# A delta-rule layer with a feed-forward: one order of the array's quarters, and 32 weight columns instead of 64 in the products between blocks

## The chip, the cores and the metric

The kernel runs on one core of a Trainium2 chip. A core has TensorE (matrix products, in the profile PE, and PEld for its weight loads), VectorE (DVE), ScalarE (ACT), GpSimd (POOL) and SyncE (SP), which issues most of the DMAs. Matmuls read SBUF and write PSUM; VectorE and ScalarE take the results from there. The metric is device time in microseconds. The kernel before takes 687.32 us, the median of three runs from 686.33 to 687.77; the profiled run has a span of 685.1 us.

## The reference

Four batches, eight heads, 768 positions, head size 48. Each head carries a 48x48 state; every position reads it with q, and then writes a corrected value with its normalised k:

```python
for t in range(S):
    kt, vt, bt = (k_n[:, :, t], v[:, :, t], beta[:, :, t, None])
    y[:, :, t] = np.einsum('bhd,bhde->bhe', q[:, :, t], state)
    v_old = np.einsum('bhde,bhd->bhe', state, kt)
    state = state + bt[:, :, :, None] * np.einsum('bhd,bhe->bhde', kt, vt - v_old)
```

The result, as 3072 tokens of 384 features, goes through a feed-forward layer: `h = x @ w_in` (384 to 2048), `g = max(h, 0) + alpha * min(h, 0)`, `g @ w_out` (back to 384). All is fp32.

## The kernel before, in words

The sequence is cut into 12 chunks of 64 positions. One step n works on one chunk of two of the four batches, so there are 24 steps; text and code call a step a batch. The 128 partitions hold two halves t (one for each of the two batches), and the eight heads are four pairs g of two parities a. A small product of 64x64 uses one quarter of the 128x128 array: the half of the partitions that it reads (array rows) and the half that it writes (array columns). Each of the four combinations of a and t goes to a quarter. `quarters()` (L377) lists the 16 products of one operation: over g, then a, then t. Which quarter (a, t) is follows from the slices: `half(t)`, `dims(a)` or `half(t ^ a)` for what is read, and the same for what is written. In `through_state` (L663) it is row a, column t; in `solve` (L683) row t, column t ^ a; in `outputs` (L695) row t ^ a, column t; in `next_state` (L710) row t ^ a, column a.

The recurrence inside a chunk becomes a triangular system for each head. Its 64x64 matrix is split into four blocks of 32 (HB = 32). The two diagonal blocks are inverted by elimination on VectorE (`eliminate`, L470 and L476), for four steps at a time; `placing` puts the inverses into `diag` and `inv`. The block between the two is found by two products: `between_1` (L623) multiplies the block outside the diagonal (`right`) by the first block's inverse and copies the result to `mid` on ScalarE (L634); `between_2` (L638) multiplies `mid` by the second inverse, and VectorE adds the result to `inv` (L650). Both ask for 64 weight columns:

```python
right[n % EARLY][half(t), a * G + g : a * G + g + 2].rearrange("p b i -> p (b i)"),
...
p[half(t), a, g], mid[n % 2][x, a * G + g], diag[n % NE][x, a * G + g, HB:C]
```

Two neighbouring blocks of 32 columns make the 64 of the first, so that the block that matters comes out in the second 32 partitions of a half; the others' results meet zeros in `diag`. Weights are the first input of `nc.tensor.matmul` after the output (L629, L644), 64 columns; the moving operand has 32.

`changes(n)` is true for n > 4: from there on odd heads change halves, and all four quarters are used. For steps 0 to 4 between_1 and between_2 use only two, upper left and lower right.

One step of the main loop is `attention(n)` (L956), in four shares: through_state(n) and between_1(n+1); solve(n), grams(n+8) and between_2(n+1); outputs(n), next_state(n) and grams for q; transposes. `weave` interleaves these shares with the feed-forward of an earlier chunk (`ffn_in` L819, `ffn_out_fast` L883), the placements, and the elimination. Orders on all engines are written out by hand: an instruction waits for what stands ahead of it on its engine. PSUM for small products is `ps_big`, three buffers in turn; the feed-forward has two banks in turn. Its evacuation is a relu on ScalarE (L829) and two multiply-adds on VectorE (L831).

Of the kernel before, what the change touches and what calls it, by code (L numbers as in the profile page):

```python
# [28 lines left out]
ALU = mybir.AluOpType  # L29
# [3 lines left out]
C = 64  # L33
HB = 32
W_IN_P = 512
BUSY = 8
EARLY = 8
# [4 lines left out]
def kernel(  # L42
# [11 lines left out]
    nc = tc.nc  # L54
# [8 lines left out]
    G = H // 2  # L63
# [23 lines left out]
    def half(i):  # L87
        return slice(64 * i, 64 * i + 64)
# [156 lines left out]
    for t in range(2):  # L245
# [5 lines left out]
        out=ones, in_=ones, compare_op=ALU.is_ge, fill=1.0, base=0,  # L251
# [7 lines left out]
    for t in range(2):  # L259
# [5 lines left out]
        out=first_of, in_=ident.rearrange("p (q u e) -> p u q e", u=2, e=HB // 2)[:, 0],  # L265
# [30 lines left out]
    NE = 2  # L296
# [77 lines left out]
        for dst, src in copies:  # L374
            nc.scalar.copy(dst.rearrange("p g i -> p (g i)"), src)  # L375

    def quarters():  # L377
        return [(g, a, t) for g in range(G) for a in range(2) for t in range(2)]

    def grams(n_k, n_q):  # L380

        p = ps_big().rearrange("p a (w g i) -> p a w g i", w=2, g=G)
        for w, n, rhs in ((0, n_k, k_t), (1, n_q, q_t)):
            if n < N:
                for g, a, t in quarters():
                    nc.tensor.matmul(  # L386
                        p[half(t ^ a if w else t), a, w, g], k_t[n][dims(a), g, half(t)],
                        rhs[n][dims(a), g, half(t)],
                    )
        if n_k < N:  # L390
            w = stats[n_k][1][:, 0:2, :, None].to_broadcast([128, 2, G, HB])
            for dst, cols in (
                (gather(n_k), slice(0, HB)), (right[n_k % EARLY][:, 1:], slice(HB, C))
            ):
                nc.vector.tensor_tensor(  # L395
                    out=dst.rearrange("p (a g) i -> p a g i", a=2), in0=p[:, :, 0, :, cols],
                    in1=w, op=ALU.mult,
                )
            keep(n_k)

        if n_q < N:
            a_t[n_q] = work.tile([128, H, C], FP32, name="a_t")
            nc.vector.tensor_tensor(
                out=a_t[n_q].rearrange("p (a g) i -> p a g i", a=2), in0=p[:, :, 1],
                in1=minus[:, None, None, :].to_broadcast([128, 2, G, C]), op=ALU.mult,
            )
# [169 lines left out]
    def changes(n):  # L576

        return n > NJ
# [41 lines left out]

    PLACING = 6

    def between_1(n):  # L623

        if n >= N:
            return
        p = ps_big()[:, :, 0 : G * HB].rearrange("p a (g i) -> p a g i", a=2, g=G)
        for g, a, t in quarters():
            nc.tensor.matmul(  # L629
                p[half(t ^ a if changes(n) else t), a, g],  # L630
                right[n % EARLY][half(t), a * G + g : a * G + g + 2].rearrange("p b i -> p (b i)"),
                diag[n % NE][half(t), a * G + g, 0:HB],
            )
        nc.scalar.copy(  # L634
            mid[n % 2].rearrange("p (a g) i -> p a g i", a=2)[:, :, :, 0:HB], p
        )

    def between_2(n):  # L638
        if n >= N:
            return  # L640
        p = ps_big()[:, :, 0 : G * HB].rearrange("p a (g i) -> p a g i", a=2, g=G)
        for g, a, t in quarters():
            x = half(t ^ a if changes(n) else t)
            nc.tensor.matmul(  # L644
                p[half(t), a, g], mid[n % 2][x, a * G + g], diag[n % NE][x, a * G + g, HB:C]
            )
        to, own = (
            x[n % NE].rearrange("p (a g) i -> p a g i", a=2)[:, :, :, HB:C] for x in (inv, diag)
        )
        nc.vector.tensor_tensor(out=to, in0=to if changes(n) else own, in1=p, op=ALU.add)  # L650


    nv, rhs_, ys, us, xts = {}, {}, {}, {}, {}
# [9 lines left out]
    def through_state(n):  # L663
        c, bp = steps[n]
        if c == 0:
            rhs_[n] = by_parity(nv[n])
            return
        r = work.tile([128, H, D], FP32, name="r")
        p = ps_big()[:, :, 0 : 2 * G * D].rearrange("p a (w g d) -> p a w g d", w=2, g=G)
        for w, x in ((0, k_t), (1, q_t)):  # L670
            for g, a, t in quarters():
                nc.tensor.matmul(  # L672
                    p[half(t), a, w, g], x[n][dims(a), g, half(t)], state[bp][dims(a), t, g]
                )
        nc.vector.tensor_tensor(  # L675
            out=r.rearrange("p (a g) d -> p a g d", a=2), in0=by_parity(nv[n]), in1=p[:, :, 0],
            op=ALU.subtract,
        )
        y = work.tile([128, H, D], FP32, name="y")
        nc.scalar.copy(by_parity(y), p[:, :, 1])  # L680
        rhs_[n], ys[n] = r.rearrange("p (a g) d -> p a g d", a=2), y

    def solve(n):  # L683
        p = ps_big()[:, :, 0 : G * D].rearrange("p a (g d) -> p a g d", a=2, g=G)
        for g, a, t in quarters():
            nc.tensor.matmul(  # L686
                p[half(t ^ a), a, g], inv[n % NE][half(t), a * G + g], rhs_[n][half(t), a, g]
            )
        us[n] = work.tile([128, 2, G, D], FP32, name="u")
        nc.vector.tensor_tensor(  # L690
            out=us[n], in0=p,
            in1=stats[n][1][:, 0:3:2, :, None].to_broadcast([128, 2, G, D]), op=ALU.mult,
        )

    def outputs(n):  # L695
        c, bp = steps[n]
        p = ps_big()[:, :, 0 : G * D].rearrange("p a (g d) -> p a g d", a=2, g=G)
        for g, a, t in quarters():
            nc.tensor.matmul(  # L699
                p[half(t), a, g], a_t[n][half(t ^ a), a * G + g], us[n][half(t ^ a), a, g]  # L700
            )
        if c == 0:
            ys[n] = work.tile([128, H, D], FP32, name="y")
            nc.scalar.copy(by_parity(ys[n]), p)
        else:
            nc.vector.tensor_tensor(
                out=by_parity(ys[n]), in0=by_parity(ys[n]), in1=p, op=ALU.add
            )

    def next_state(n):  # L710
        c, bp = steps[n]
        if c < NCH - 1:
            p = ps_big()[:, :, 0 : G * D].rearrange("p t (g d) -> p t g d", g=G)
            for g, a, t in quarters():
                nc.tensor.matmul(  # L715
                    p[dims(a), t, g], k_late[n % NKL][half(t ^ a), 2 * g + a, 0:D],
                    us[n][half(t ^ a), a, g],
                )
            for a in range(2):
                x = state[bp][dims(a)]  # L720
                nc.vector.tensor_tensor(out=x, in0=x, in1=p[dims(a)], op=ALU.subtract)  # L721
# [315 lines left out]
    def queries():  # L1037

        p = [x.rearrange("p (n g i) -> p n g i", n=2, g=G) for x in ffn_banks]
        for n in range(2):  # L1040
            for g, a, t in quarters():
                nc.tensor.matmul(
                    p[a][half(t ^ a), n, g], k_t[n][dims(a), g, half(t)],
                    q_t[n][dims(a), g, half(t)],
                )
            a_t[n] = work.tile([128, H, C], FP32, name="a_t")
# [259 lines left out]
```

## Time and profile before

| engine | busy us | share | instructions |
|---|---|---|---|
| TensorE matmul (PE) | 664.0 | 97% | 10063 |
| TensorE weight load (PEld) | 573.3 | 84% | 10063 |
| VectorE (DVE) | 461.9 | 67% | 1133 |
| ScalarE (ACT) | 248.8 | 36% | 592 |

| group | count | busy us |
|---|---|---|
| feed-forward in, L819 | 1152 | 269.1 |
| between_1, L629 | 768 | 17.6 |
| between_2, L644 | 768 | 17.4 |
| solve, L686 (both forms) | 768 | 16.4 |
| outputs, L699 | 768 | 16.5 |
| copy to mid, L634 | 24 | 0.38 each |
| sum into inv, L650 | 24 | 0.41 each |

An fp32 matmul shows as two recorded instructions, each with its own weight load, so 24 steps of 16 products are 768; a transpose shows as one. A form such as `64*64 64x32` is array rows * weight columns, and then the output. A row of the timeline merges neighbours of one kind: start, length, engine, line, count; matmuls overlap, so what a group costs is the next group's start less its own. Brackets give idle time of the engine ahead of it and what ended it.

### The profile page before, as it was taken

How to read it: one execution, taken by the hardware profiler on the slowest of the kernel's cores; microseconds unless marked ns; L12 is line 12 of the kernel's file. 1: busy time of each engine (PE TensorE's matmuls, PEld its weight loads, DVE VectorE, ACT ScalarE, POOL GpSimd, SP SyncE). 2: the span in 40 equal slices, each digit the busy share in tenths (PEclk: the TensorE clock that was granted, in tenths of full speed). 3: DMA queues.
4: the chain of work that ended last, by engine and by line, in shares of the span. 5: the costliest groups of instructions: out<-in, count | busy, mean ns of one | idle time of the engine just before them, and what ended most of it. 6: DMA issues, size and time to landing. Idle time of an engine off the chain costs nothing.

```text
span 685.1 us, 22945 instructions
## 1 busy us (share of the span) xinstructions
PE 664.0 (97%) x10063; PEld 573.3 (84%) x10063; DVE 461.9 (67%) x1133; ACT 248.8 (36%) x592; POOL 19.2 (3%) x74
## 2 busy tenths in 40 slices
PE   6989999999999999999999999999999999999997
PEld 4567877666678988988988988988989989989997
DVE  5875799879988378967368967369877255245161
ACT  5936756344434244244234234134034133131110
POOL 4000010000000000000000000000000000000000
PEclk9999999999999999999999999999999999999999
DMA  8847644211412212212212112211211210100000
GB/s 123 237 139 197 161 106 117 69 36 37 78 30 39 40 36 45 41 34 46 37 37 37 36 26 36 38 27 34 48 22 28 54 27 17 31 7 2 24 1 23
DMA packets 110963, 37.76 MB, mean 55 GB/s; under 512 B 104160, under 2 KB 107248, under 8 KB 110864
## 3 DMA queue, kind: packets, MB, share of 16 engines
q1 hardware_dynamic: 109088, 35.81, 24.2%
q8 instruction: 79, 1.29, 0.8%
q10 hardware_dynamic: 1776, 0.49, 0.4%
q14 instruction: 20, 0.16, 0.1%
HBM read 31.56 MB, written 4.72 MB: 53 GB/s over the span
## 4 chain that ended last, share of the span: by engine, by line
PE 82%; DVE 11%; ACT 3%; DMA 1%; issue 1%; ACTq 0%; SPq 0%; DVEq 0%
PE p_ffn L819 35%; PE p_ffn L883 27%; PE p_big L672 3%; PE p_big L386 3%; PE p_big L353 2%; PE p_big L699 2%; PE p_big L686 2%; PE p_big L629 2%; PE p_big L644 2%; DVE block L476 2%; DVE prod L470 2%; DMA ke<-in_k_dram 1%; PE p_big L715 1%; PE p_ffn L861 1%; DVE block L446 1%
## 5 line engine op out<-in xcount | busy, mean ns | idle before, releaser
L819 PE MATMUL p_ffn<-xt,w_in 128*128 128x256 f32 x1152 | 269.1, 385 | 5.1 <-DVE act L831 2.1
L819 PEld LDWEIGHTS p_ffn<-xt,w_in 128*128 128x128 f32 x1152 | 211.8, 190 | 36.1 <-issue 3.6
L831 DVE SCALAR_TENSOR_TENSOR act<-act,al_t,p_ffn 128x256 f32<-128x256 f32 x176 | 76.3, 474 | 71.1 <-ACT act L829 70.7
L829 ACT ACTIVATE act<-p_ffn 128x512 f32<-128x512 f32 x88 | 52.3, 594 | 124.6 <-PE p_ffn L819 124.5
L883 PE MATMUL p_ffn<-w_out,act 128*128 128x192 f32 x480 | 83.7, 328 | 0.0
L883 PEld LDWEIGHTS p_ffn<-w_out,act 128*128 128x128 f32 x480 | 78.6, 190 | 0.9
L476 DVE TENSOR_TENSOR block<-block,prod 128x30 f32<-128x30 f32 (+9 forms) x150 | 49.7, 331 | 5.1
L470 DVE TENSOR_TENSOR prod<-block 128x30 f32<-128x30 f32 (+9 forms) x150 | 48.7, 325 | 2.0
L903 DVE TENSOR_TENSOR o_sb<-u,p_ffn 128x192 f32<-128x192 f32 x40 | 13.2, 351 | 41.7 <-PE p_ffn L883 35.4
L680 ACT COPY y<-p_big 128x384 f32<-128x384 f32 x22 | 10.5, 478 | 69.5 <-DVE r L675 69.5
L375 ACT COPY q_t<-p_big 128x512 f32<-128x512 f32 x24 | 13.9, 589 | 55.8 <-PE p_big L353 55.8
L375 ACT COPY k_t<-p_big 128x512 f32<-128x512 f32 x24 | 13.9, 578 | 54.5 <-PE p_big L353 54.4
L883 PE MATMUL p_ffn<-space_out,sums 128*128 128x192 f32 x160 | 29.3, 326 | 0.0
L883 PE MATMUL p_ffn<-more,sums 128*128 128x192 f32 x160 | 29.3, 326 | 0.0
L883 PE MATMUL p_ffn<-w_out,sums 128*128 128x192 f32 x160 | 27.7, 326 | 0.0
L883 PEld LDWEIGHTS p_ffn<-more,sums 128*128 128x128 f32 x160 | 26.6, 190 | 0.0
L883 PEld LDWEIGHTS p_ffn<-space_out,sums 128*128 128x128 f32 x160 | 26.6, 190 | 0.0
L594 ACT ACTIVATE diag<-inverse,which 64x128 f32<-64x128 f32 (+2 forms) x62 | 25.5, 412 | 2.2 <-DVE inverse L446 1.3
L883 PEld LDWEIGHTS p_ffn<-w_out,sums 128*128 128x128 f32 x160 | 25.8, 190 | 0.0
L434 ACT COPY same<-right 32x256 f32<-32x256 f32 x32 | 12.9, 402 | 34.5 <-DVE right L395 34.4
L721 DVE TENSOR_TENSOR state<-state,p_big 48x384 f32<-48x384 f32 x44 | 24.1, 549 | 1.3 <-PE p_big L715 0.9
L903 DVE TENSOR_TENSOR u<-u,p_ffn 128x192 f32<-128x192 f32 x20 | 7.0, 351 | 25.4 <-PE p_ffn L883 25.4
(155 smaller groups left out, 945.7 us busy)
## 6 DMA issues: line engine op xcount, KB each, us to landing
w_out<-in_moe_w_in_dram SPq DMA_DIRECT2D x12, 512.0 KB, 4.9
qp<-in_q_dram SPq DMA_DIRECT2D x48, 96.0 KB, 3.0
v_raw<-in_v_dram SPq DMA_DIRECT2D x48, 96.0 KB, 3.0
kl<-in_k_dram SPq DMA_DIRECT2D x96, 48.0 KB, 2.6
out_dram<-o_sb SPq DMA_DIRECT2D x92, 48.0 KB, 1.6
space_out<-in_moe_w_out_dram SPq DMA_DIRECT2D x11, 384.0 KB, 4.3
ke<-in_k_dram SPq DMA_DIRECT2D x43, 96.0 KB, 3.5
w_out<-in_moe_w_out_dram SPq DMA_DIRECT2D x5, 384.0 KB, 4.8
```

What stands on the lines that cost most here:

```text
L375: nc.scalar.copy(dst.rearrange("p g i -> p (g i)"), src)
L386: nc.tensor.matmul(p[half(t ^ a if w else t), a, w, g], k_t[n][dims(a), g, half(t)], rhs[n][dims(a), g, half(t)],)
L470: nc.vector.tensor_tensor(out=prod, in0=r[:, 0:j, j : j + 1].to_broadcast([128, j, n]), in1=r[:, j : j + 1, j + 1 : HB].to_broadcast([128, ...
L476: nc.vector.tensor_tensor(out=r[:, 0:j, j + 1 : HB], in0=r[:, 0:j, j + 1 : HB], in1=prod, op=ALU.add)
L594: nc.scalar.mul(dst[n % NE][to or rows, a.start * G : a.stop * G, cols], src[m][rows, heads], which[rows, i : i + 1],)
L672: nc.tensor.matmul(p[half(t), a, w, g], x[n][dims(a), g, half(t)], state[bp][dims(a), t, g])
L721: nc.vector.tensor_tensor(out=x, in0=x, in1=p[dims(a)], op=ALU.subtract)
L819: nc.tensor.matmul(p_h[:, i], w_in[:, t, (f + i) * 128 : (f + i + 1) * 128], xt[:, t], start=(t == 0), stop=(t == KT - 1),)
L829: nc.scalar.activation(g, p_h, ACT.Relu, scale=-1.0)
L831: nc.vector.scalar_tensor_tensor(out=g[:, i], in0=g[:, i], scalar=al_t[:, f + i : f + i + 1], in1=p_h[:, i], op0=ALU.mult, op1=ALU.add,)
L883: nc.tensor.matmul(p, x(i), w(i), start=(i == 0), stop=(i == FP - 1))
L903: nc.vector.tensor_tensor(out=to, in0=x, in1=p, op=ALU.add)
```

## The change

`quarters` now takes two functions, which say what array row and what array column (a, t) has, and sorts the 16 products of an operation by g, row, column. All small products so walk the quarters in one order. For steps 0 to 4, where between_1 and between_2 use two quarters, the sorted order takes each twice in a row.

From step 5 on, between_1 loads only the block that matters, 32 weight columns, and writes only the second 32 partitions of each half; between_2 loads 32 columns of mid and writes only the first 32 partitions. The copy to mid and the sum into inv then touch 32 partitions of each half, so each becomes two instructions. It is meant to shorten weight loads, and to have successive products find free quarters. The arithmetic of what is kept is the same.

```diff
--- before.py
+++ after.py
@@ -374,15 +374,28 @@
         for dst, src in copies:
             nc.scalar.copy(dst.rearrange("p g i -> p (g i)"), src)
 
-    def quarters():
-        return [(g, a, t) for g in range(G) for a in range(2) for t in range(2)]
+    def quarters(row, col):
+
+        return sorted(
+            ((g, a, t) for g in range(G) for a in range(2) for t in range(2)),
+            key=lambda x: (x[0], row(x[1], x[2]), col(x[1], x[2])),
+        )
+
+    def parity(a, t):
+        return a
+
+    def batch_(a, t):
+        return t
+
+    def mixed(a, t):
+        return t ^ a
 
     def grams(n_k, n_q):
 
         p = ps_big().rearrange("p a (w g i) -> p a w g i", w=2, g=G)
         for w, n, rhs in ((0, n_k, k_t), (1, n_q, q_t)):
             if n < N:
-                for g, a, t in quarters():
+                for g, a, t in quarters(parity, mixed if w else batch_):
                     nc.tensor.matmul(
                         p[half(t ^ a if w else t), a, w, g], k_t[n][dims(a), g, half(t)],
                         rhs[n][dims(a), g, half(t)],
@@ -620,34 +633,60 @@
 
     PLACING = 6
 
+    def first_half(t):
+        return slice(64 * t, 64 * t + HB)
+
+    def second_of(t):
+        return slice(64 * t + HB, 64 * t + C)
+
     def between_1(n):
 
         if n >= N:
             return
         p = ps_big()[:, :, 0 : G * HB].rearrange("p a (g i) -> p a g i", a=2, g=G)
-        for g, a, t in quarters():
-            nc.tensor.matmul(
-                p[half(t ^ a if changes(n) else t), a, g],
-                right[n % EARLY][half(t), a * G + g : a * G + g + 2].rearrange("p b i -> p (b i)"),
-                diag[n % NE][half(t), a * G + g, 0:HB],
-            )
-        nc.scalar.copy(
-            mid[n % 2].rearrange("p (a g) i -> p a g i", a=2)[:, :, :, 0:HB], p
-        )
+        to = mid[n % 2].rearrange("p (a g) i -> p a g i", a=2)[:, :, :, 0:HB]
+
+        if changes(n):
+            for g, a, t in quarters(batch_, mixed):
+                nc.tensor.matmul(
+                    p[second_of(t ^ a), a, g], right[n % EARLY][half(t), a * G + g + 1],
+                    diag[n % NE][half(t), a * G + g, 0:HB],
+                )
+            for t in range(2):
+                nc.scalar.copy(to[second_of(t)], p[second_of(t)])
+        else:
+            for g, a, t in quarters(batch_, batch_):
+                x = right[n % EARLY][half(t), a * G + g : a * G + g + 2]
+                nc.tensor.matmul(
+                    p[half(t), a, g], x.rearrange("p b i -> p (b i)"),
+                    diag[n % NE][half(t), a * G + g, 0:HB],
+                )
+            nc.scalar.copy(to, p)
 
     def between_2(n):
         if n >= N:
             return
         p = ps_big()[:, :, 0 : G * HB].rearrange("p a (g i) -> p a g i", a=2, g=G)
-        for g, a, t in quarters():
-            x = half(t ^ a if changes(n) else t)
-            nc.tensor.matmul(
-                p[half(t), a, g], mid[n % 2][x, a * G + g], diag[n % NE][x, a * G + g, HB:C]
-            )
         to, own = (
             x[n % NE].rearrange("p (a g) i -> p a g i", a=2)[:, :, :, HB:C] for x in (inv, diag)
         )
-        nc.vector.tensor_tensor(out=to, in0=to if changes(n) else own, in1=p, op=ALU.add)
+        if changes(n):
+            for g, a, t in quarters(mixed, batch_):
+                x = half(t ^ a)
+                nc.tensor.matmul(
+                    p[first_half(t), a, g], mid[n % 2][x, a * G + g, 0:HB],
+                    diag[n % NE][x, a * G + g, HB:C],
+                )
+            for t in range(2):
+                x = to[first_half(t)]
+                nc.vector.tensor_tensor(out=x, in0=x, in1=p[first_half(t)], op=ALU.add)
+        else:
+            for g, a, t in quarters(batch_, batch_):
+                nc.tensor.matmul(
+                    p[half(t), a, g], mid[n % 2][half(t), a * G + g],
+                    diag[n % NE][half(t), a * G + g, HB:C],
+                )
+            nc.vector.tensor_tensor(out=to, in0=own, in1=p, op=ALU.add)
 
 
     nv, rhs_, ys, us, xts = {}, {}, {}, {}, {}
@@ -668,7 +707,7 @@
         r = work.tile([128, H, D], FP32, name="r")
         p = ps_big()[:, :, 0 : 2 * G * D].rearrange("p a (w g d) -> p a w g d", w=2, g=G)
         for w, x in ((0, k_t), (1, q_t)):
-            for g, a, t in quarters():
+            for g, a, t in quarters(parity, batch_):
                 nc.tensor.matmul(
                     p[half(t), a, w, g], x[n][dims(a), g, half(t)], state[bp][dims(a), t, g]
                 )
@@ -682,7 +721,7 @@
 
     def solve(n):
         p = ps_big()[:, :, 0 : G * D].rearrange("p a (g d) -> p a g d", a=2, g=G)
-        for g, a, t in quarters():
+        for g, a, t in quarters(batch_, mixed):
             nc.tensor.matmul(
                 p[half(t ^ a), a, g], inv[n % NE][half(t), a * G + g], rhs_[n][half(t), a, g]
             )
@@ -695,7 +734,7 @@
     def outputs(n):
         c, bp = steps[n]
         p = ps_big()[:, :, 0 : G * D].rearrange("p a (g d) -> p a g d", a=2, g=G)
-        for g, a, t in quarters():
+        for g, a, t in quarters(mixed, batch_):
             nc.tensor.matmul(
                 p[half(t), a, g], a_t[n][half(t ^ a), a * G + g], us[n][half(t ^ a), a, g]
             )
@@ -711,7 +750,7 @@
         c, bp = steps[n]
         if c < NCH - 1:
             p = ps_big()[:, :, 0 : G * D].rearrange("p t (g d) -> p t g d", g=G)
-            for g, a, t in quarters():
+            for g, a, t in quarters(mixed, parity):
                 nc.tensor.matmul(
                     p[dims(a), t, g], k_late[n % NKL][half(t ^ a), 2 * g + a, 0:D],
                     us[n][half(t ^ a), a, g],
@@ -1038,7 +1077,7 @@
 
         p = [x.rearrange("p (n g i) -> p n g i", n=2, g=G) for x in ffn_banks]
         for n in range(2):
-            for g, a, t in quarters():
+            for g, a, t in quarters(parity, mixed):
                 nc.tensor.matmul(
                     p[a][half(t ^ a), n, g], k_t[n][dims(a), g, half(t)],
                     q_t[n][dims(a), g, half(t)],
```

## The prediction

> **What bounds the kernel now.** I read the page first, for engine totals and the chain that ended last.
>
> ```profile
> PE 664.0 (97%) x10063; PEld 573.3 (84%) x10063; DVE 461.9 (67%) x1133; ACT 248.8 (36%) x592; POOL 19.2 (3%) x74
> PE 82%; DVE 11%; ACT 3%; DMA 1%; issue 1%; ACTq 0%; SPq 0%; DVEq 0%
> ```
>
> TensorE fills 97% of the span and 82% of the chain. An average over stages hides where it is not the limit, so next came busy time in two stretches.
>
> ```profile
> 155.00:213.00 58.00, 54.25 (x1031) 40.91 (x1029) 52.67 (x131) 24.98 (x65) 2.44 (x8) 1.00 0.28 50
> 213.00:637.00 424.00, 423.78 (x6378) 387.09 (x6379) 274.85 (x650) 131.30 (x317) 3.44 (x16) 1.00 0.17 32
> ```
>
> After the stretch, its length come PE, PEld, DVE, ACT and POOL busy. From 213 to 637 us PE is busy 423.78 of 424 us; its only listed wait there is 0.6 us. A nanosecond saved on PE in it is a nanosecond of the end. From 155 to 213 us DVE is busy 52.67 of 58 and PE stands still 3.75: there DVE work counts. Batch 5's between-products start at 170.94 us, batch 6's at 187.05, batch 7's at 215.21. So of the 19 batches that change (5 to 23), 17 lie in the PE-bound part, with two products each: **34 products that count**.
>
> Then the timeline, for what one product costs. Each product is 16 small matmuls, which the profile records as 32 pairs of LDWEIGHTS and MATMUL (two per fp32 matmul).
>
> ```profile
> 446.49 0.56 PEld L672 LDWEIGHTS p_big<-state,k_t 48*64 48x64 f32 x32 [0.23 <-issue]
> 446.95 0.56 PEld L672 LDWEIGHTS p_big<-state,q_t 48*64 48x64 f32 x32
> 447.41 0.56 PEld L629 LDWEIGHTS p_big<-diag,right 64*64 64x64 f32 x32
> 448.02 4.61 PEld L819 LDWEIGHTS p_ffn<-xt,w_in 128*128 128x128 f32 x22
> ...
> 452.96 0.56 PEld L686 LDWEIGHTS p_big<-r,inv 64*64 64x64 f32 x32 [0.33 <-issue]
> 453.42 0.56 PEld L644 LDWEIGHTS p_big<-diag,mid 64*64 64x64 f32 x32
> ```
>
> Subtract starts. L672 already walks the quarters in the new order: 446.49 to 446.95, 0.46 us for 32 pairs. L686 walks them crosswise (upper left, lower right, then the other two): 452.96 to 453.42, also 0.46. The order of four different quarters costs nothing. L629 takes 447.41 to 448.02, 0.61: the same 0.46 plus **0.15 us** until the array takes 128x128 weights. Where the moving operand has 64 columns (L386) the pitch is again about 0.46-0.48; where the weights have 48 columns (L715) it is 0.36. So the columns of the weights set the pitch, not those that stream.
>
> ```profile
> 51.50 0.34 PEld L545 LDWEIGHTS p_big<-turned,sums 32*32 32x32 f32 x32 [0.33 <-issue]
> 51.87 0.30 PEld L819 LDWEIGHTS p_ffn<-xt,w_in 128*128 128x128 f32 x2
> ...
> 74.47 1.01 PEld L644 LDWEIGHTS p_big<-diag,mid 64*64 64x64 f32 x32 [0.33 <-issue]
> 75.52 1.16 PEld L819 LDWEIGHTS p_ffn<-xt,w_in 128*128 128x128 f32 x6
> ```
>
> L545 loads 32 columns into four separate parts of the array, between two stretches of feed-forward: 51.50 to 51.87, **0.37 us** with its own start and its leaving. L644 at 74.47 is batch 2 or 3, which uses two quarters only: 1.05 us, not 0.61, since two quarters share the loads of four.
>
> **What the Trainium skill says.** "TensorE: Matmul & The Clock Gate", section LDWEIGHTS: the load takes time by its columns, columns / 1.2 ns, rows don't matter. For 64 and 32 columns that is 53 and 27 ns. The trace agrees: 0.46 us / 8 rounds of four quarters is 58 ns a round, and the 48-column 0.36 / 8 is 45. "TensorEngine Tiling (Array Packing)", Key Properties: "Changing tiling mode (not just tile) drains the TensorE"; Available Configurations lists 64x32 apart from 64x64. The trace shows such a drain between 64x64 and 128x128 (the 0.15), none between 64x64 and 64x32, since no instruction has 32 columns with 64 rows. The first page's Engine queue depths gives TensorE a window of 64 from which loads are pulled ahead. That four quarters run side by side although each matmul is two recorded pairs fits it; how far it reaches past one quarter's queue no row shows.
>
> **The change part by part.**
>
> *32 columns.* It removes half the weight columns of 34 products that count. Today each takes 0.61 from first load to the feed-forward's first load; with 32 columns I take L545's 0.37: **-0.24**. That is the nearest row: same weight columns, four parts busy; its streams are 16 columns, not 32, but streamed columns did not set the pitch.
>
> *A new switch.* Today L629 follows L672, and L644 follows L386 or L686, in the same 64x64 tiling. After the change the array goes 64x64, 64x32, 128x128. The new switch costs between 0, if the hardware lets the tilings mix, and 0.15, what leaving 64x64 costs now. I take 0.15, because of the skill's sentence. Each product then gains 0.24 - 0.15 = 0.09, and 34 of them **-3.1 us**; without the drain 34 x 0.24 = -8.2.
>
> *Split evacuations.* The copy to mid (L634) and the sum into inv (L650) each become two instructions on 32 partitions. Splitting partitions halves nothing: 128x256 takes L634 0.38, and L434 copies 32x256 in 0.40. So 19 more instructions on ACT and 19 on DVE. From 213 us both hide under PE: ACT is busy 131 of 424 us and DVE 275; behind the second copy on ACT stand the diag placements and the relu L829, behind the second sum on DVE stands the scaling L658, and a feed-forward bank has some 2.6 us (12 recorded matmuls of 0.22) before PE wants it again, against 1.5 for its relu and two sums. In the DVE-bound part the chain has these:
>
> ```profile
> 177.94 0.33 DVE inv L650
> ...
> 190.92 0.28 ACT mid L634
> ...
> 195.80 0.33 DVE inv L650
> ```
>
> Two more sums at 0.33 and one copy of about 0.3: at most 1.0, at least 0 where a gap swallows them. I take **+0.8**.
>
> *Order, four quarters.* grams for q, solve, outputs, next_state, queries: **0**, by the two equal 0.46.
>
> *Order, batches 0 to 4.* Here the new order is upper left twice, lower right twice, where it alternated. If loads pass each other freely it costs nothing; if a quarter's queue holds only one waiting pair, the second quarter starts two rounds (0.12 us) late and ends as late. Ten products, some back to back: 0 to 1.2 us, of which part hides behind ScalarE. I take **+0.4**.
>
> *Sum:* -3.1 + 0.8 + 0.4 = -1.9, and 687.3 - 1.9 = **685.4 us**.
>
> **The rivals.**
>
> *No drain, 680.3 us:* -8.2 + 1.2 = -7.0. For it: 48-row and 48-column products follow the 64x64 ones with no gap (0.36 and 0.46). Against: those use the same quarters, so they are no change of tiling; and the one change the trace shows is paid for every time.
>
> *Eaten up, about 687.3:* the drain takes 0.15, the exit is no cheaper, and DVE in the stretch before 213 us hands on more than two sums. Each product would gain 0.05, 1.7 in all, against 1.2 to 1.8 lost. For it: the gain is a difference of two nearly equal terms. Against: L545's exit is inside its 0.37.
>
> *Slower, 693 us or so, in two ways.* If 64-row tiles with 32 columns load no faster than 64-column ones, 34 products pay the 0.15 for nothing: +5.1 + 1.2, 693.6. No row shows that shape; the 48-column 0.36 speaks against it. Or the doubled quarters of batches 0 to 4 run one after the other: ten products of 1.05 become about 2.0, +9.4, and 687.3 - 3.1 + 0.8 + 9.4 = 694.4. Against it: each matmul is already two pairs in one quarter, and two quarters still overlap.
>
> **How the numbers follow.** Forecast 0.56, no drain 0.22, eaten up 0.08, slower 0.14. The forecast is the likeliest case. Its own bounds are 687.3 - 3.1 + 0 = 684.2 and 687.3 - 3.1 + 2.2 = 686.4. The range must take in the no-drain case, so its low end is 680.0; the high end 688.0 covers eaten up and leaves out the slower cases, 0.14, and a little of the other tails. Two parts in a thousand are 1.4 us: faster means under 685.9. The no-drain case (0.22) and about three quarters of the forecast (0.42) lie there: 0.64. Within: 0.14 of the forecast and eaten up: 0.22. Slower: 0.14.
>
> **What would show it.** Loads of L629's and L644's successors should have the form 64*32 from batch 5 on. The timeline between the last L672 load's group and the next L819 is the test: L672's second group would stretch from 0.46 to about 0.61 (drain), and the new product to feed-forward take 0.37. If L672 stays at 0.46, the no-drain rival holds. If the new product takes 0.6, the slower one does. Starts of L686, L699, L715 to their successors should stay 0.46, 0.46, 0.36. L644 of batches 2 and 3 should stay near 1.05, at worst 1.2; near 2 means that the doubled order serializes. The 213 to 637 stretch should shrink by some 3 us with PE still without waits, and 155 to 213 grow by under 1. Any PE wait on L831 after 213 us would mean that the split evacuations do not hide, and the prediction is wrong there.

## The result, and the profile after

The changed kernel takes **690.39 us** (median of 4 runs, 690.21 to 692.47) against 687.55 us (686.33 to 687.82) for the kernel before, run beside it: a ratio of 1.0052, 95% interval 1.0029 to 1.0074. The forecast was 685.4 us with a range up to 688.0; the change makes the kernel slower.

First the page of the kernel after, the engine totals and the chain by engine:

```profile
PE 663.9 (96%) x10063; PEld 568.9 (83%) x10063; DVE 471.2 (68%) x1152; ACT 259.9 (38%) x611; POOL 19.4 (3%) x74
PE 78%; DVE 13%; ACT 4%; SPq 2%; issue 1%; DMA 1%; DVEq 0%; ACTq 0%
```

PEld fell from 573.3 to 568.9, so weights are loaded faster, as meant. DVE grew by 9.3 us and ACT by 11.1 us, with 19 more instructions each. The chain gives TensorE 78% where it gave 82%, VectorE 13% where it gave 11%. Now the same two stretches of the kernel after:

```profile
155.00:213.00 58.00, 52.45 (x1024) 38.64 (x1023) 52.38 (x129) 25.72 (x66) 1.50 (x6) 1.00 0.24 45
213.00:637.00 424.00, 421.63 (x6367) 381.21 (x6366) 284.41 (x669) 141.40 (x335) 4.50 (x18) 1.00 0.17 33
```

PE stands still for 2.4 us of the long stretch; before it was 0.2 us. In the short one it stands still for 5.6 us, where it was 3.75. These are the waits of TensorE after 213 us, from the list of waits of PE and of the weight loads:

```profile
PE p_ffn L922 <- DVE act L870: 1.0, 2, 0.5
PE p_ffn L858 <- issue: 0.7, 1, 0.7
PE p_ffn L858 <- DVE act L870: 0.6, 1, 0.6
```

```profile
PEld p_ffn L922 <- DVE act L870: 2.0, 3, 0.8
```

The second line is one moment near 320 us in which TensorE got no instruction. Only the third was there before (as L819 on L831). The first is new: `ffn_out_fast`'s product (L922; L883 before) waits for `act`, the multiply-adds of L870 (L831 before), at about 274, 378 and 480 us. The prediction had named such a wait as what would prove it wrong, but had followed only the buffers of `ffn_in`.

**Where the time went.** Matching the matmuls of the two traces by their operands and subtracting starts: at 156 us the kernel after is 0.50 us late, a difference of the start-up that varies from run to run. At 214 us it is 2.44 us late, at 663 us 3.27 us. So 1.93 us are lost between 156 and 214 us, and 0.83 us in the rest. In the rest the three waits of L922 cost 0.76 + 0.75 + 0.37 = 1.88 us, and the moment near 320 us 0.50 us more than before (every kernel here shows between nothing and a microsecond there, before 0.3). Nine small losses of 0.04 to 0.08 us between the products come to 0.52, and the 32 products themselves gain 2.07. The parts are 1.93 + 1.88 + 0.50 + 0.52 - 2.07 = 2.76 us; the medians differ by 2.8.

The small losses have one place that can be read without an offset, in a kernel below that changes only between_2, from batch 8 on. TensorE comes to 251 us 0.06 us earlier than in the kernel before, but the weight load behind VectorE's multiply-adds starts at 251.48 us, where it started at 251.49, and 0.04 of the 0.06 is gone. That suggests that VectorE sets this moment, and that a gain ahead of it is handed back. The other losses were not followed up.

### The profile page after: what moved, and what is told of

Same layout as the page of the kernel before. It is cut to its first block, busy times and chain, and to the rows that moved or that the text cites. A ratio compares the mean times of both kernels' runs of the same rounds, so it can differ in the third digit from the quotient of the medians.

```text
span 688.4 us, 22971 instructions
## 1 busy us (share of the span) xinstructions
PE 663.9 (96%) x10063; PEld 568.9 (83%) x10063; DVE 471.2 (68%) x1152; ACT 259.9 (38%) x611; POOL 19.4 (3%) x74
## 3 DMA queue, kind: packets, MB, share of 16 engines
q8 instruction: 79, 1.29, 0.8%
## 4 chain that ended last, share of the span: by engine, by line
PE 78%; DVE 13%; ACT 4%; SPq 2%; issue 1%; DMA 1%; DVEq 0%; ACTq 0%
PE p_ffn L858 32%; PE p_ffn L922 26%; PE p_big L711 2%; PE p_big L353 2%; PE p_big L399 2%; DVE block L489 2%; DVE prod L483 2%; PE p_big L738 2%; PE p_big L725 2%; PE p_big L1028 2%; DVE act L870 2%; SPq L119 1%; PE p_big L754 1%; PE p_big L676 1%; ACT diag L607 1%
## 5 line engine op out<-in xcount | busy, mean ns | idle before, releaser
L870 DVE SCALAR_TENSOR_TENSOR act<-act,al_t,p_ffn 128x256 f32<-128x256 f32 x176 | 76.3, 475 | 72.9 <-ACT act L868 72.6
L922 PE MATMUL p_ffn<-w_out,act 128*128 128x192 f32 x480 | 84.7, 329 | 1.1 <-DVE act L870 1.0
L922 PEld LDWEIGHTS p_ffn<-w_out,act 128*128 128x128 f32 x480 | 78.4, 190 | 3.1 <-DVE act L870 2.0
L483 DVE TENSOR_TENSOR prod<-block 128x30 f32<-128x30 f32 (+9 forms) x150 | 48.8, 325 | 2.0
L922 PE MATMUL p_ffn<-space_out,sums 128*128 128x192 f32 x160 | 29.3, 326 | 0.0
L922 PE MATMUL p_ffn<-more,sums 128*128 128x192 f32 x160 | 29.3, 326 | 0.0
L922 PE MATMUL p_ffn<-w_out,sums 128*128 128x192 f32 x160 | 27.7, 326 | 0.0
L922 PEld LDWEIGHTS p_ffn<-space_out,sums 128*128 128x128 f32 x160 | 26.5, 190 | 0.0
L922 PEld LDWEIGHTS p_ffn<-more,sums 128*128 128x128 f32 x160 | 26.5, 190 | 0.0
L922 PEld LDWEIGHTS p_ffn<-w_out,sums 128*128 128x128 f32 x160 | 25.8, 190 | 0.0
```

The costliest lines, as they stand in the source:

```text
L483: nc.vector.tensor_tensor(out=prod, in0=r[:, 0:j, j : j + 1].to_broadcast([128, j, n]), in1=r[:, j : j + 1, j + 1 : HB].to_broadcast([128, ...
L870: nc.vector.scalar_tensor_tensor(out=g[:, i], in0=g[:, i], scalar=al_t[:, f + i : f + i + 1], in1=p_h[:, i], op0=ALU.mult, op1=ALU.add,)
L922: nc.tensor.matmul(p, x(i), w(i), start=(i == 0), stop=(i == FP - 1))
```

## The array did what was forecast

The timeline of weight loads of the kernel after, where the prediction showed L672, L629, L686 and L644 (L711, L651, L725 and L676 now):

```profile
450.68 0.56 PEld L711 LDWEIGHTS p_big<-state,q_t 48*64 48x64 f32 x32
451.30 0.34 PEld L651 LDWEIGHTS p_big<-diag,right 64*32 64x32 f32 x32
451.69 4.62 PEld L858 LDWEIGHTS p_ffn<-xt,w_in 128*128 128x128 f32 x22
456.63 0.56 PEld L725 LDWEIGHTS p_big<-r,inv 64*64 64x64 f32 x32 [0.33 <-issue]
457.24 0.34 PEld L676 LDWEIGHTS p_big<-diag,mid 64*32 64x32 f32 x32
457.63 0.94 PEld L858 LDWEIGHTS p_ffn<-xt,w_in 128*128 128x128 f32 x5
```

L725 to L676 takes 0.61, where 0.46 stood: the drain costs 0.15, as chosen. The product itself takes 0.39 to the feed-forward, where 0.61 stood and 0.37 was taken. Together 1.00 against 1.07: **0.07 us gained per product**, not 0.09. Over all 32 products the matched matmuls give 0.07 for each between_1, and for between_2 0.055 up to 428 us, where it follows the products of `grams`, and 0.07 from 453 us on, where it follows `solve`. This agrees with the Trainium skill ("TensorEngine Tiling (Array Packing)", Key Properties: a change of the tiling mode drains TensorE); from the last 64x64 matmul to the first 64x32 the trace has 148 ns, where the last 64x64 product and the next stood 38 apart before.

## Experiments

Ratios are to the kernel before, run beside it on the same chip. Profiles are compared from 156 us on, since start-up moves whole runs by a microsecond or more.

### The order alone

```diff
 (after, all batches: 64 columns, one copy, one sum, as before)
-                    p[second_of(t ^ a), a, g], right[n % EARLY][half(t), a * G + g + 1],
+                    p[half(t ^ a), a, g], x.rearrange("p b i -> p (b i)"),
...
-            for t in range(2):
-                nc.scalar.copy(to[second_of(t)], p[second_of(t)])
+            nc.scalar.copy(to, p)
```

> The changed kernel with 64 weight columns, one copy to mid and one sum into inv in every batch again; only the order of the quarters is new. Theory A (the second copy on ScalarE delays the relu, its two multiply-adds and then TensorE) and theory B (the second sum on VectorE does it): the time of before, 687.3 within 0.7. Theory C (the order itself costs): slower by 2 us or more, near 690. The doubled quarters of batches 0 to 4 should cost at most some tenths.

Measured: 686.61 us against 687.07, ratio 1.0009 (0.9988 to 1.0031). From 156 to 214 us its matmuls keep their distance to those of the kernel before within 0.02 us, and no wait is new. **The order costs nothing that shows**, also where two quarters are used twice in a row: in the kernel after, the product of an early batch that took 1.05 us takes 1.07.

### The two evacuations, each alone, with 64 columns

Here each evacuation is cut into two halves of 64 partitions.

```diff
 (before; copy)
-        nc.scalar.copy(
-            mid[n % 2].rearrange("p (a g) i -> p a g i", a=2)[:, :, :, 0:HB], p
-        )
+        to = mid[n % 2].rearrange("p (a g) i -> p a g i", a=2)[:, :, :, 0:HB]
+        for x in [half(0), half(1)] if changes(n) else [slice(0, 128)]:
+            nc.scalar.copy(to[x], p[x])
```

> The kernel before, with nothing changed but that from batch 5 on the copy to mid is two instructions of 64 partitions each. Theory A: slower by 2 to 5 us, 689.5 to 692, with the waits of the changed kernel (TensorE at the first feed-forward product for the multiply-adds in batches 8, 12, 16, and the loss from 185 to 203 us), since there is no gain on TensorE to set against them. Theory B: within 0.7 of before.

```diff
 (before; sum)
-        nc.vector.tensor_tensor(out=to, in0=to if changes(n) else own, in1=p, op=ALU.add)
+        if changes(n):
+            for x in (half(0), half(1)):
+                nc.vector.tensor_tensor(out=to[x], in0=to[x], in1=p[x], op=ALU.add)
+        else:
+            nc.vector.tensor_tensor(out=to, in0=own, in1=p, op=ALU.add)
```

> The kernel before, with nothing changed but that from batch 5 on the sum into inv is two instructions of 64 partitions each. Theory B: slower by 2 us or more, near 690. Theory A: about 0.5 us for each of the two batches before 213 us, so 687.3 to 688.5, and no new wait of TensorE after 213 us.

Measured: two copies 688.94 us, ratio 1.0019 (1.0004 to 1.0034); two sums 689.07, ratio 1.0033 (1.0008 to 1.0059). With TensorE's work unchanged, each split evacuation alone makes the kernel slower, the copies by a little less than the 2 us expected. (What the expectations call the first feed-forward product is the `ffn_out_fast` product; their batches 8, 12 and 16 are 10, 14 and 18.) The two copies bring the waits of the `ffn_out_fast` product for `act` after 213 us (0.6 us in two) and lose 0.6 us before it. The two sums bring no wait for `act` of the `ffn_out_fast` product. By 186 us they have lost 2.5 us: 0.8 up to the end of the wait for y (2.1 us, where it was 1.5), and 1.7 in some 3 us at half clock behind it. At 198 us the next wait is shorter, and 0.5 comes back, which leaves 2.0. After 214 us they lose only at the moment near 320 us.

### What a split evacuation costs

Step 13, around 372 us, in the kernel before: ScalarE's instructions from the copy of y to the last relu, the multiply-adds that need that relu, and the `ffn_out_fast` product that needs those.

```profile
371.70 0.48 ACT L680 COPY y<-p_big 128x384 f32<-128x384 f32 x1 [2.32 <-DVE r L675]
372.07 0.38 ACT L634 COPY mid<-p_big 128x256 f32<-128x256 f32 x1
372.33 1.24 ACT L594 ACTIVATE diag<-inverse,which 128x128 f32<-128x128 f32 x3
372.51 2.76 PE L883 MATMUL p_ffn<-w_out,act 128*128 128x192 f32 x16
373.48 0.57 ACT L829 ACTIVATE act<-p_ffn 128x512 f32<-128x512 f32 x1
374.09 0.87 DVE L831 SCALAR_TENSOR_TENSOR act<-act,al_t,p_ffn 128x256 f32<-128x256 f32 x2 [0.36 <-ACT act L829]
```

And in the kernel after:

```profile
374.87 0.48 ACT L719 COPY y<-p_big 128x384 f32<-128x384 f32 x1 [2.32 <-DVE r L714]
375.36 0.74 ACT L656 COPY mid<-p_big 32x256 f32<-32x256 f32 x2
375.61 2.44 PE L922 MATMUL p_ffn<-w_out,act 128*128 128x192 f32 x14
376.11 1.23 ACT L607 ACTIVATE diag<-inverse,which 128x128 f32<-128x128 f32 x3
377.36 0.60 ACT L868 ACTIVATE act<-p_ffn 128x512 f32<-128x512 f32 x1
377.99 0.87 DVE L870 SCALAR_TENSOR_TENSOR act<-act,al_t,p_ffn 128x256 f32<-128x256 f32 x2 [1.10 <-ACT act L868]
378.53 0.59 PE L922 MATMUL p_ffn<-w_out,act 128*128 128x192 f32 x2 [0.48 <-DVE act L870]
```

A copy of 0.38 us doesn't cost ScalarE 0.38 us. Before, the copy starts 0.37 after y's, whose length is 0.48, and the placements start 0.26 after it: neighbours overlap by some 0.11. The two copies on 32 partitions start only when y's is over, and take 0.75 to the placements. From y's start to the placements it is 0.63 before and 1.24 after, **0.61 us more**. The relu starts 1.78 after y's copy before, 2.49 after; the multiply-adds wait 1.10 for it where they waited 0.36. Before, the `ffn_out_fast` product of 16 matmuls ran through without a gap; now its last two wait for those multiply-adds. On VectorE one sum takes 0.33 to the next instruction's start (177.86 to 178.19 in the kernel before), the pair 0.87 (178.26 to 179.13 in the kernel after): **0.5 us more**.

Is it the second instruction that costs, or the partitions? The same kernel before, with each evacuation cut along the free axis instead, two times 128 partitions by 128 elements:

```diff
 (before)
-        nc.scalar.copy(
-            mid[n % 2].rearrange("p (a g) i -> p a g i", a=2)[:, :, :, 0:HB], p
-        )
+        to = mid[n % 2].rearrange("p (a g) i -> p a g i", a=2)[:, :, :, 0:HB]
+        for x in range(2) if changes(n) else [slice(0, 2)]:
+            nc.scalar.copy(to[:, x], p[:, x])
...
+            for x in range(2):
+                nc.vector.tensor_tensor(out=to[:, x], in0=to[:, x], in1=p[:, x], op=ALU.add)
```

> The kernel before; from batch 5 on the copy to mid and the sum into inv are two instructions each, as after, but cut along the free axis: 128 partitions by 128 elements, twice. It tells what makes the split evacuations dear. Theory (an instruction on other partitions than its neighbours can't overlap with them): these overlap; an ACT copy of 384 elements lasts 0.48 and of 256 lasts 0.38, so one of 128 some 0.28 with a pitch of about 0.17, the pair some 0.35 from the first copy to the placements, where the pair on 32 partitions took 0.75; the two sums some 0.40, where 0.83 was taken; no wait of the ffn_out_fast product for act after 213 us; 687.2 to 687.8, within 0.1% of the kernel before. Rival (it is one more instruction that costs, whatever partitions it is on): pair of copies 0.6 or more, pair of sums 0.7 or more, waits at 376 us, 688.5 to 689.5.

Measured: 687.95 us against 687.74, ratio 1.0007 (0.9989 to 1.0026). Its timelines of ScalarE at step 13 and of VectorE in step 6:

```profile
374.94 0.48 ACT L684 COPY y<-p_big 128x384 f32<-128x384 f32 x1 [2.33 <-DVE r L679]
375.31 0.44 ACT L636 COPY mid<-p_big 128x128 f32<-128x128 f32 x2
375.63 1.25 ACT L594 ACTIVATE diag<-inverse,which 128x128 f32<-128x128 f32 x3
```

```profile
199.13 0.48 DVE L652 TENSOR_TENSOR inv<-inv,p_big 128x128 f32<-128x128 f32 x2
199.52 0.55 DVE L662 TENSOR_TENSOR v_raw<-v_raw,norm 128x384 f32<-128x384 f32 x1
```

Two copies take 0.32, two sums 0.39, against 0.75 and 0.87 on 32 partitions; there is no wait of the `ffn_out_fast` product after 213 us, and against the kernel before it stands at the end within 0.02 us where it stood at 156 us (VectorE's full stretch costs 0.2, the moment near 320 us happened to be shorter by 0.3). So it isn't the number of instructions. A copy cut across the partitions keeps the whole one's rows of 256 elements and lasts nearly as long (0.36 us against 0.38), so the second copy adds a full distance, 0.26 of the 0.61; cut lengthwise it adds 0.05. The other 0.35 is overlap lost three times, at 0.11 to 0.12 each: **the partitions, which differ from the neighbours', take the overlap away.** For VectorE the Trainium skill says so ("VectorE: DVE Perf Modes", section Two Vector instructions with no wait between them): in its model, an instruction whose input or output starts in another quadrant of partitions than the last one in that memory is held until all earlier ones have finished. The first sum starts at partition 0 like its neighbours and overlaps (0.33 behind L408); the second, from partition 64, and the scaling behind it, from 0 again, are held: 0.41 and 0.45. For ScalarE, "ScalarE: Activation LUTs" (What ACT_TABLE_LOAD costs) has back-to-back ACTIVATEs overlap by some 93 ns; here full-height copies overlap by 0.10 to 0.12 us, those on 32 partitions, which start at 32 and 96, by none, and the instruction behind them neither. The page doesn't speak of partitions. The kernel above with two copies of 64 partitions tells whether their number counts or where they start:

```profile
372.24 0.48 ACT L680 COPY y<-p_big 128x384 f32<-128x384 f32 x1 [2.32 <-DVE r L675]
372.62 0.75 ACT L636 COPY mid<-p_big 64x256 f32<-64x256 f32 x2
373.38 1.22 ACT L594 ACTIVATE diag<-inverse,which 128x128 f32<-128x128 f32 x3
```

Its first copy starts at partition 0, like y's, and follows y's after 0.38 us, as the full-height one did (0.37). The second, from partition 64, and the placement behind it, from 0 again, follow after 0.38 each, their whole length. In the kernel after the first copy starts at partition 32, and follows y's only after 0.49. So it is the partition where an instruction starts that decides, on ScalarE as on VectorE, in the cases measured here.

### The copies moved behind the relu

```diff
 (after; the two copies are issued at the head of the next share)
-            for t in range(2):
-                nc.scalar.copy(to[second_of(t)], p[second_of(t)])
+            def copies(to=to, p=p):
+                for t in range(2):
+                    nc.scalar.copy(to[second_of(t)], p[second_of(t)])
+
+            late_copies[n] = copies
...
         yield
+        copy_late(n + 1)
         solve(n)
```

> The changed kernel with its two copies to mid issued at the head of the next share, behind the placements and the relu on ScalarE; the same instructions, another place in the queue. Theory A: the waits at the first feed-forward product go, 2 us or more come back, 686 to 688.3. Theory B and theory C: about 690.4 as before.

Measured: 690.21 us, ratio 1.0045 (1.0030 to 1.0061). From 155 us on the waits of the `ffn_out_fast` product for `act` are gone, which shows that the relu's place behind the copies made them. In their stead between_2 waits for mid:

```profile
PE p_big L685 <- ACT mid L657: 3.7, 6, 1.7
```

A wait was exchanged for another: the copies have to be done between the relu and between_2, and there is no room for both. So the time that was expected to come back didn't. The longest of these waits, 1.7 us at 177 us, is followed by 3 us in which TensorE is granted half its clock (more on that below).

### One product at a time

```diff
 (after; between_1 alone: between_2 has 64 columns and one sum again)
-                    p[first_half(t), a, g], mid[n % 2][x, a * G + g, 0:HB],
+                    p[half(t), a, g], mid[n % 2][x, a * G + g],
...
-            for t in range(2):
-                x = to[first_half(t)]
-                nc.vector.tensor_tensor(out=x, in0=x, in1=p[first_half(t)], op=ALU.add)
+            nc.vector.tensor_tensor(out=to, in0=to, in1=p, op=ALU.add)
```

> The changed kernel with 32 columns in between_1 alone (two copies to mid); between_2 loads 64 columns again and has one sum. Theory D (the costs of the two splits and the gain on TensorE add up: copy +1.9 us, sum +2.0, and about 0.065 us gained for each of 17 products of a kind that count, 1.1): 687.1 + 1.9 - 1.1 = 687.9, with waits at the first feed-forward product in batches 8, 12 and 16. Theory E (the costs come only from both splits together): within 0.7 of 686.

The other kernel, between_2 alone, has 64 columns and one copy again in between_1, as in the kernel with the order alone.

> The changed kernel with 32 columns in between_2 alone (two sums into inv); between_1 loads 64 columns again and has one copy. Theory D: 687.1 + 2.0 - 1.1 = 688.0, the loss from 155 to 213 us, and after 213 us a gain without new waits of TensorE. Theory E: within 0.7 of 686.

Measured: between_1 alone 689.18 us, ratio 1.0022 (1.0001 to 1.0043), with the waits of the `ffn_out_fast` product (1.0 us in two). Between_2 alone 687.94, ratio 1.0010 (0.9989 to 1.0031), without them. The first lies above the expected 687.9, the second at the expected 688.0. From 156 to 214 us the first loses 0.55 and the second 1.40 us; the sum, 1.95, is the 1.93 of both together. After 214 us the first loses 0.68 and the second nothing on balance: its gain is used up by the moment near 320 us, longer here by 0.7.

### From which batch on

The prediction's batch numbers were off by one: `attention(n)` issues between_1(n+1), so that the product at 156.85 us is batch 5's and the one at 215.21 batch 8's. Two kernels carried that mistake: they keep batches 5 and 6 as before, and were meant to keep out all that lies before 213 us, but split batch 7.

```diff
 (after; between_1 and between_2 alike; the new branch has 64 columns and one evacuation)
-        if changes(n):
+        if changes(n) and not (n > 6):
...
+        elif changes(n):
```

> The changed kernel, but 32 columns and both splits only from batch 7 on; batches 5 and 6, whose products lie in the stretch where VectorE sets the pace, keep 64 columns, one copy and one sum. Theory D by stage: the loss of about 2 us before 213 us goes, the waits at the first feed-forward product in batches 8, 12 and 16 stay (some 2 us) and eat the gain of 2.2: 687 to 688.3. Theory F (the splits cost TensorE's stretch nothing, all is lost before 213 us): 685.0.

```diff
 (the same; in between_1 also)
+        if changes(n) and not (n > 6 and n % NJ != 1):
```

> As e10, and batches 9, 13, 17 and 21 keep 64 columns and one copy in between_1, which lies ahead of the relu that the first feed-forward product waits for. Theory D by stage: those waits go, 13 + 17 products gain 0.065 us each, 2.0 in all: 685.1 within 0.7, under the kernel before. If it stays at 687 or more, the waits come from elsewhere.

Measured: 689.62 us, ratio 1.0047 (1.0013 to 1.0081), and 690.82, ratio 1.0048 (1.0034 to 1.0062). Both missed what they were built for: the loss before 213 us was still there, and in the second the waits at 272 and 376 us too, since the batches left out are the wrong ones. They show something else: batch 7 alone, whose step is the last in which VectorE is full, loses 3.0 us between 186 and 214 us. The same cut, one batch later:

```diff
+        if changes(n) and not (n > 7):
```

> The kernel after, with the 32 columns, the two copies and the two sums only from between_1(8) on (attention(7), 215 us); batches 5, 6 and 7 keep 64 columns, one copy and one sum, in the new order. Theory (the loss is in two places, batches 5 to 7 beside VectorE's full stretch, and three waits of the ffn_out_fast product for act behind the two copies, in batches 10, 14 and 18): the 2.5 us lost before 214 us are gone, 32 products gain 0.065 each = 2.1 us, and the three waits with what they push cost some 1.6 to 2; 686.5 to 687.5, beside 687.4 for the kernel before, with waits of 0.3 to 0.8 us at 272 and 376 us in the profile. Rival (the split evacuations cost in every batch, also where TensorE is the bound): 689 to 690.

Measured: 688.76 us against 687.23, ratio 1.0021 (0.9999 to 1.0044); its profiled run spans 687.1 us. Above the expected 686.5 to 687.5, below the rival's 689. The interval takes in 1. In its profile nothing is lost from 156 to 214 us (0.01 us); from there on it loses 0.9 us, with the three waits of the `ffn_out_fast` product, as the kernel after does. Batch 7 in this kernel (one copy, one sum), ScalarE, VectorE and TensorE from the timeline:

```profile
191.78 0.38 ACT L656 COPY mid<-p_big 128x256 f32<-128x256 f32 x1
193.21 0.57 ACT L884 ACTIVATE act<-p_ffn 128x512 f32<-128x512 f32 x1
193.81 0.87 DVE L886 SCALAR_TENSOR_TENSOR act<-act,al_t,p_ffn 128x256 f32<-128x256 f32 x2 [0.55 <-ACT act L884]
196.68 0.41 DVE L688 TENSOR_TENSOR inv<-inv,p_big 128x256 f32<-128x256 f32 x1
198.34 0.87 DVE L886 SCALAR_TENSOR_TENSOR act<-act,al_t,p_ffn 128x256 f32<-128x256 f32 x2
199.36 2.40 PE L874 MATMUL p_ffn<-xt,w_in 128*128 128x256 f32 x10 [0.97 <-DVE prod L483]
```

and in the kernel that splits from batch 7 on:

```profile
190.41 0.74 ACT L664 COPY mid<-p_big 32x256 f32<-32x256 f32 x2
192.42 0.60 ACT L884 ACTIVATE act<-p_ffn 128x512 f32<-128x512 f32 x1
193.05 0.87 DVE L886 SCALAR_TENSOR_TENSOR act<-act,al_t,p_ffn 128x256 f32<-128x256 f32 x2 [1.29 <-ACT act L884]
195.92 0.83 DVE L698 TENSOR_TENSOR inv<-inv,p_big 32x256 f32<-32x256 f32 x2
198.20 0.87 DVE L886 SCALAR_TENSOR_TENSOR act<-act,al_t,p_ffn 128x256 f32<-128x256 f32 x2
199.22 3.60 PE L874 MATMUL p_ffn<-xt,w_in 128*128 128x256 f32 x10 [2.32 <-DVE prod L483]
```

The late relu leaves VectorE idle for 1.29 us instead of 0.55 in the stretch in which it is the bound (+0.74), the two sums add 0.5, and TensorE waits 2.32 instead of 0.97 us for the next multiply-adds (the row names L483, the instruction just behind them on VectorE). Then the same ten matmuls take 3.60 us instead of 2.40. The stretches of this kernel from before the wait's end to 3 us behind it (granted clock is the third column from the right):

```profile
198.50:200.50 2.00, 1.28 (x6) 1.12 (x7) 1.93 (x7) 0.00 (x1) 0.00 (x0) 0.94 0.00 0
200.50:203.50 3.00, 3.00 (x34) 2.06 (x36) 0.76 (x2) 0.00 (x0) 0.00 (x0) 0.50 0.00 0
203.50:205.00 1.50, 1.50 (x82) 1.41 (x75) 1.08 (x3) 0.00 (x0) 0.00 (x0) 0.94 0.00 0
```

The clock granted to TensorE is 0.50 for 3 us: a wait of 1.35 us more becomes a loss of nearly 3. In the profile of the kernel after the same wait of 2.32 us at 200.8 us was followed by no such drop, and the loss there, from 193 to 201 us, was 1.55 us.

### A version that gains

The waits of the `ffn_out_fast` product fall in batches 10, 14 and 18. One kernel keeps 64 columns and one copy in every fourth batch of between_1, one leaves between_1 as it was:

```diff
 (between_1)
+        if changes(n) and not (n > 7 and n % NJ != 2):
 (between_2)
+        if changes(n) and not (n > 7):
```

> The same, but between_1 also keeps 64 columns and its one copy in batches 10, 14, 18 and 22, where the elimination stands on VectorE between the copy and the last multiply-adds. Theory: no wait for act at 272, 376 and 476 us; 12 products of between_1 and 16 of between_2 at 0.065 each = 1.8 us gained, nothing lost; 685.3 to 686, faster than the kernel before. Rival (those waits move to other batches or to another buffer): within 0.3 us of the kernel with both from batch 8 on.

The other, with 64 columns in every batch of between_1:

```diff
 (between_1)
+        if changes(n) and not (False):
 (between_2)
+        if changes(n) and not (n > 7):
```

> Only between_2 with 32 columns and two sums, from batch 8 on; between_1 keeps 64 columns and one copy throughout. Theory (after 213 us the two sums hide, only the two copies are seen): 16 products at 0.065 = 1.0 us gained, no new wait; 686.1 to 686.7. Rival (two sums cost VectorE's queue 0.5 us a batch and TensorE waits for act or u later): 687.5 or more.

Measured: the first **685.54 us** against 687.23, ratio 0.9976 (0.9956 to 0.9996); the second 686.24, ratio 0.9982 (0.9968 to 0.9996). Both are as the theory had it, and both faster than the kernel before, with intervals that end just under 1, and so than the kernel after. The first in step 13, where the kernel after waited:

```profile
372.24 0.38 ACT L656 COPY mid<-p_big 128x256 f32<-128x256 f32 x1
372.67 2.77 PE L938 MATMUL p_ffn<-w_out,act 128*128 128x192 f32 x16
373.65 0.57 ACT L884 ACTIVATE act<-p_ffn 128x512 f32<-128x512 f32 x1
374.25 0.87 DVE L886 SCALAR_TENSOR_TENSOR act<-act,al_t,p_ffn 128x256 f32<-128x256 f32 x2 [0.36 <-ACT act L884]
```

The 16 matmuls run through, as before. From 214 us on its profile gains 1.2 us on the kernel before, 1.4 without the moment near 320 us: 0.050 for each of its 28 products, net of the small losses between them. The second gains 0.7 so counted, 0.046 for each of 16.

## Why the prediction was wrong

- **32 columns, -0.24, and a new switch, +0.15:** right in kind. The drain is there and costs what was taken. The net gain was put at 0.09 and is 0.055 to 0.07: the product with its exit takes 0.39, not 0.37. L545, the row chosen, leaves its tiling sooner: 107 ns from its last matmul to the feed-forward's first, where the new product takes 122.
- **34 products that count:** 32. The numbering was one batch off, so three batches, not two, lie where VectorE is full, and the third is the one with least room.
- **Sum of the gain, -3.1:** 32 products gain 2.07, and the small losses between them take 0.5 of it back, so -1.6. That each nanosecond saved on PE from 213 us on is one of the end held for three quarters of them: a busy share of PE doesn't show such moments.
- **Order, four quarters, 0:** right. **Order, batches 0 to 4, +0.4:** the order costs nothing, so this term was too careful.
- **Split evacuations, +0.8, the step that failed.** It took the added cost of a copy as 0.3 and of a sum as 0.33, the distance of a full-height one to the next. That is the share of the second instruction alone. It left out the overlap that is lost where the partitions change, and the cost is 0.61 and 0.5. The kernel before showed it, in the two state sums on 48 partitions (1.11 us for a pair, 0.56 apart). Instead of "at most 1.0", the stretch before 213 us lost 1.93 net, some 2.2 before the gain of its six products.
- **"From 213 us both hide under PE" failed too.** It was argued from busy shares and from how soon a feed-forward bank is wanted again. The consumer that counts is another: the last relu's `act` is read by the last matmuls of the `ffn_out_fast` product, and in the steps with elimination on VectorE that product had run on with hardly any room. Three such waits cost 1.88 us, where the prediction had nothing. The kernel with late copies takes these waits away; the one that keeps one copy in those batches shows that 28 of 32 products can be had without them.
- **The rivals.** "Eaten up" was nearest: its mechanism (each product gains some 0.05, and VectorE hands on more than two sums) is what happened, but with a loss of 1.2 to 1.8 where some 4.1 was measured (2.2 before 214 us and 1.9 at the three waits). The two slower cases didn't occur: loads of 32 columns are faster, and doubled quarters don't serialize.

What stays open: what stands behind the other small losses between the products; what the pause near 320 us is; how much of the 2.0 us of the two sums is left without the drop of the clock; and whether a single evacuation at full height over the 32-column result would keep the whole gain. It would read PSUM rows that no product has written, and wasn't tried.

## What to carry to other kernels

Cost an instruction on a busy queue by the distance to its neighbours' starts, not by its length, and expect one that starts at another partition than its neighbours to lose the overlap on both sides; here an evacuation was cut in two along the free axis for 0.05 us, and across the partitions for 0.5 to 0.6. Where an edit lengthens a queue off the critical path, follow every item behind it to its consumer on the bound engine, not only the buffer that it frees. And a saving of 0.06 us per use can be kept if it is applied only where the added work has room.

## What the runs showed of the hardware that was not expected

- The cost of the partitions above: copies on 32 partitions start 0.375 to 0.39 us apart and don't overlap with a full-height neighbour; behind a full-height one of the same row length the next instruction starts after 0.263.
- After an idle time of TensorE of about 2.1 to 2.3 us (1.7 us in one case) the granted clock can fall to 0.50 for some 3 us. It did so in the profiles of the two kernels split from batch 7 on, in the one with two sums and in the one with late copies, and not in that of the kernel after, with the same idle time of 2.32 us, nor in that of between_2 alone, with 2.1, nor after the waits of 1.7 us in those of the kernel after and of between_1 alone. The Trainium skill ("TensorE: Matmul & The Clock Gate", Part 1) describes such a gate with a free-running window of about 3.4 us, which would fit that the same wait is punished in one run and not in another; that it is the reason, no run here shows. Here less idle time than such a window was enough.
